# Sigmoid attention and a SwiGLU block on one core: from one head at a time to units of four heads, two side by side in the array

## The chip, the core and the metric

The kernel runs on one core of a Trainium2 chip. A core has a matrix engine (TensorE, PE in the profile; its weight loads are the rows PEld), VectorE (DVE), ScalarE (ACT), GpSimd (POOL) and SyncE (SP), and 16 DMA engines between its memory SBUF and the chip's main memory. Matrix products land in PSUM, eight banks of 2 KB in each of 128 partitions. The metric is the device time of one execution in microseconds.

## The reference, cut to what matters

```python
# q, k, v: (8, 12, 448, 64) float32 ; w_gate, w_val: (768, 1536) ; w_out: (1536, 768)
scores = scale * np.matmul(q, k.transpose(0, 1, 3, 2)) - np.log(S)      # scale = 1/8, S = 448
attn   = 1.0 / (1.0 + np.exp(-scores))                                  # sigmoid, no softmax
attn_out = np.matmul(attn, v)                                           # per batch and head
x = attn_out.transpose(0, 2, 1, 3).reshape(3584, 768)
g = x @ w_gate
silu = g * (1.0 / (1.0 + np.exp(-g)))
out = (silu * (x @ w_val)) @ w_out                                      # (3584, 768) float32
```

## The kernel before, in words

The work goes by batch. Three stages of three batches overlap: in pass `g` the attention of batch `g`, the first feed-forward products (FFN-1: gate and value) of batch `g-1` and the second (FFN-2) of batch `g-2` are written in turns, one head, one column block `f` of FFN-1 and one FFN-2 half per inner step `j` (12 steps a pass). The Tile scheduler then orders the instructions of each engine by its own priorities, so what stands on an engine is not quite what is written.

Tokens are cut into four chunks of 112. `emit_load` (L106) loads a chunk of q, k or v of all twelve heads with one DMA on SyncE's queue; the runs in main memory are 64 floats, 256 bytes. GpSimd casts to 16 bits (L116; for batch 0 ScalarE does, L114). `emit_tr` (L125) transposes q or k of a pair of heads by four TensorE products with the identity into the PSUM buffer `TO`, and VectorE copies it out (L132): a pair's q lies then with one head in partitions 0 to 63 and the other in 64 to 127.

Scores (`emit_qk`, L151): per head four products, one for each chunk of keys, each with 64 rows of contraction (one half of the array's rows) and 112 columns of weights, moving 448 queries. All four of a head use the same half. ScalarE takes the sigmoid out of PSUM (L163, 112x448). `emit_pv` (L168): per head four products with 112 rows and 64 columns of weights (one half of the array's columns, always the first), accumulated into `ps_pv`; VectorE casts them into the half of `xT` that belongs to the head (L185).

FFN-1 (`emit_ffn1_mm`, L194): per block `f` six products for the gate and six for the value, 128x128 weights, 448 moving. ScalarE takes the sigmoid of the gate (L205), VectorE multiplies twice (L207, L209). FFN-2 (`emit_ffn2`, L223): per 112 tokens and 384 output columns twelve products into `TO`, moving 384; ScalarE copies out (L230), and GpSimd's queue stores 112 rows (L235). Transposes and FFN-2 share the one buffer `TO`.

Weights come as 36 tiles of 128x768 floats (L81) through four staging buffers, three at each step, and are cast by ScalarE (L88) and VectorE (L90) in turns.

Of the kernel before, what the change touches and what calls it, by code (L numbers as in the profile page):

```python
# [9 lines left out]
FP32 = mybir.dt.float32  # L10
FP16 = mybir.dt.float16
# [7 lines left out]
def kernel(  # L19
# [15 lines left out]
    PC = 112  # L35
    NC_ = S // PC
    NP = H // 2
    NF = DFF // 128
    HSC = 4096.0
# [5 lines left out]
    psum = ctx.enter_context(tc.tile_pool(name="ps", bufs=1, space=bass.MemoryType.PSUM))  # L45
    stg = ctx.enter_context(tc.tile_pool(name="stg", bufs=1))
    one = ctx.enter_context(tc.tile_pool(name="one", bufs=1))
    two = ctx.enter_context(tc.tile_pool(name="two", bufs=2))
    wp = ctx.enter_context(tc.tile_pool(name="wp", bufs=1))
    attn = ctx.enter_context(tc.tile_pool(name="attn", bufs=4))  # L50
    ptp = ctx.enter_context(tc.tile_pool(name="ptp", bufs=8))
    xtp = ctx.enter_context(tc.tile_pool(name="xtp", bufs=12))
    htp = ctx.enter_context(tc.tile_pool(name="htp", bufs=22))
    osp = ctx.enter_context(tc.tile_pool(name="osp", bufs=2))

    idn = one.tile([PC, PC], BF16, tag="idn")
    make_identity(nc, idn)
    sb_t = one.tile([128, 1], FP32, tag="sbiast")
    nc.gpsimd.memset(sb_t, sbias)

    wg16 = [wp.tile([128, DFF], FP16, tag=f"wg{j}", name=f"wg16_{j}") for j in range(NP)]
    wv16 = [wp.tile([128, DFF], FP16, tag=f"wv{j}", name=f"wv16_{j}") for j in range(NP)]
    wo16 = [wp.tile([128, DM], FP16, tag=f"wo{f}", name=f"wo16_{f}") for f in range(NF)]

    wjobs = []
    for j in range(NP):
        rows = slice(j * 128, (j + 1) * 128)
        for h2 in range(2):
            cols = slice(h2 * DM, (h2 + 1) * DM)
            wjobs.append((moe_w_gate[rows, cols], wg16[j][:, cols]))  # L70
            wjobs.append((moe_w_val[rows, cols], wv16[j][:, cols]))
    for f in range(NF):
        rows = slice(f * 128, (f + 1) * 128)
        wjobs.append((moe_w_out[rows, :], wo16[f][:, :]))
    NWJ = len(wjobs)
    wstage = {}

    def emit_wload(i):
        src, _ = wjobs[i]
        st = stg.tile([128, DM], FP32, tag="wst", bufs=4, name=f"wst{i}")  # L80
        nc.sync.dma_start(out=st, in_=src)  # L81
        wstage[i] = st

    def emit_wcast(i, eng=None):
        _, dst = wjobs[i]
        eng = eng or nc.scalar
        if eng is nc.scalar:
            eng.copy(out=dst, in_=wstage.pop(i))  # L88
        else:
            eng.tensor_copy(out=dst, in_=wstage.pop(i))  # L90

    q16 = {}
    k16 = {}
    v16 = {}

    def get16(d, b, dt, nm):
        if b not in d:
            d[b] = two.tile([PC, NC_, H, D], dt, tag=nm, name=f"{nm}{b}")
        return d[b]

    def emit_load(b, which, c):
        src = (q, k, v)[which]
        nm = ("qst", "kst", "vst")[which]
        st = stg.tile([PC, H, D], FP32, tag=nm, bufs=(4, 4, 3)[which], name=f"{nm}_{b}_{c}")
        sl = slice(c * PC, (c + 1) * PC)
        nc.sync.dma_start(out=st, in_=src[b][:, sl, :].rearrange("h t d -> t h d"))  # L106
        return st

    def emit_cast(b, which, c, st, eng=None):
        d, dt, nm = ((q16, BF16, "q16"), (k16, BF16, "k16"), (v16, FP16, "v16"))[which]  # L110
        t = get16(d, b, dt, nm)
        eng = eng or nc.gpsimd
# [245 lines left out]
```

## Time and profile before

| | before |
|---|---|
| three runs | 640.72, 641.11, 647.34 us (median 641.11) |
| span of the profiled execution | 646.1 us, 5.0 above the median |
| busy: PE, PEld | 610.1, 297.3 us |
| busy: ACT, DVE, POOL | 321.8, 220.9, 85.9 us |
| moved by DMA | 58.71 MB, 131648 packets under 512 bytes |
| products on PE | 3072 |

A row of the timeline has the start, the time from its first start to its last end, the engine, the line, the operation with its tiles (out<-in, contraction*columns of the weights, shape of the moving operand), and how many instructions it merges; in brackets is the idle time before it and what ended it. Products are pipelined: a single one lasts 0.35 us from start to end while the next starts 0.19 us after it, so starts, and not ends, give the pace. A row of the windows has, for a stretch of time, the busy time and the number of instructions of each engine, the granted TensorE clock, the mean share of the DMA engines and the GB/s.

### The profile page before, as it was taken

To read this page: it belongs to the slowest core of one execution; us is meant where nothing else is said; L and a number is where in the kernel's file an instruction comes from. 1 tells how busy PE (TensorE), PEld (TensorE's weight loads), DVE (VectorE), ACT (ScalarE), POOL (GpSimd) and SP (SyncE) were. 2 spreads that over 40 slices of the span, in tenths; PEclk is the share of its full clock that TensorE was granted. 3 is DMA by queue.
4 is the path that set the end of the run, shared out by engine and by line. 5 is a ranking of instruction groups with operands and counts; after the bars stand their busy time and mean duration, and the time that the engine had idled before them with its cause. 6 is when DMAs were issued, how large, how long until landed. Compare 5 with 4: busy or idle time off the path is not lost.

```text
span 646.1 us, 7821 instructions
## 1 busy us (share of the span) xinstructions
PE 610.1 (94%) x3072; PEld 297.3 (46%) x3072; DVE 220.9 (34%) x402; ACT 321.8 (50%) x576; POOL 85.9 (13%) x123
## 2 busy tenths in 40 slices
PE   0899879999999999999999999999999999999985
PEld 0332323344555455444555455544545454546653
DVE  0232326444333432344333433344333433333310
ACT  4767537655545554455445554555445544542221
POOL 0011110351231102210040102110000000000000
PEclk9999999999999999999999999999999999999999
DMA  9956986995695423704092400010010000000112
GB/s 191 203 144 164 231 243 186 208 208 106 137 218 117 102 50 78 136 23 85 22 173 62 87 23 21 22 30 14 22 43 22 1 23 21 22 22 22 44 43 65
DMA packets 138341, 58.71 MB, mean 91 GB/s; under 512 B 131648, under 2 KB 131648, under 8 KB 138304
## 3 DMA queue, kind: packets, MB, share of 16 engines
q1 hardware_dynamic: 135744, 47.19, 35.3%
q0 software_dynamic: 2560, 11.01, 5.5%
q8 instruction: 24, 0.39, 0.3%
q14 instruction: 13, 0.11, 0.1%
HBM read 47.19 MB, written 11.01 MB: 90 GB/s over the span
## 4 chain that ended last, share of the span: by engine, by line
PE 60%; issue 32%; POOL 2%; ACT 2%; SPq 1%; DMA 1%; DVE 1%; POOLq 0%; ACTq 0%
PE ps_sc L151 12%; PE ps_g L194 12%; PE ps_pv L168 12%; PE ps_vl L194 11%; PE ps_o L223 10%; PE ps_tr L125 4%; SPq L106 1%; POOL out_dram L235 1%; DMA kst<-in_k_dram 1%; ACT pt L163 1%; POOL v L116 0%; DVE xT L185 0%; DVE kT L132 0%; ACT wg L88 0%; ACT L163 0%
## 5 line engine op out<-in xcount | busy, mean ns | idle before, releaser
L163 ACT ACTIVATE pt<-ps_sc,sb_t 112x448 f16<-112x448 f32 x384 | 222.4, 636 | 102.2 <-PE ps_sc L151 93.0
L223 PE MATMUL ps_o<-wo,hT 128*112 128x384 f16 x768 | 135.7, 326 | 4.2 <-ACT osb L230 4.2
L194 PE MATMUL ps_g<-xT,wg 128*128 128x448 f16 x576 | 131.7, 361 | 2.2 <-DVE t L207 1.3
L194 PE MATMUL ps_vl<-xT,wv 128*128 128x448 f16 x576 | 129.3, 359 | 0.3 <-DVE t L207 0.3
L151 PE MATMUL ps_sc<-qT,kT 64*112 64x448 bf16 x384 | 121.9, 409 | 2.9 <-ACT pt L163 2.8
L223 PEld LDWEIGHTS <-hT 128*112 128x112 f16 x768 | 99.8, 130 | 35.4 <-issue 5.6
L168 PE MATMUL ps_pv<-pt,v 112*64 112x448 f16 x384 | 110.2, 390 | 1.6 <-ACT pt L163 1.2
L207 DVE TENSOR_TENSOR t<-ps_g,s 128x448 f16<-128x448 f32 x96 | 60.0, 625 | 149.0 <-ACT s L205 148.8
L205 ACT ACTIVATE s<-ps_g 128x448 f16<-128x448 f32 x96 | 52.2, 544 | 91.1 <-PE ps_g L194 89.5
L230 ACT ACTIVATE osb<-ps_o 112x384 f32<-112x384 f32 x64 | 31.4, 491 | 113.5 <-PE ps_o L223 113.5
L194 PEld LDWEIGHTS <-wg 128*128 128x128 f16 x576 | 50.0, 99 | 72.3 <-issue 35.5
L194 PEld LDWEIGHTS <-wv 128*128 128x128 f16 x576 | 50.0, 98 | 68.2 <-issue 31.2
L185 DVE CAST xT<-ps_pv 64x448 f16<-64x448 f32 x96 | 59.3, 617 | 61.0 <-PE ps_pv L168 60.3
L209 DVE SCALAR_TENSOR_TENSOR hT<-ps_vl,t 128x448 f16<-128x448 f32 x96 | 60.0, 625 | 46.7 <-PE ps_vl L194 44.6
L235 POOL DMA_DIRECT2D out_dram<-osb x32 | 17.0, 531 | 364.6 <-ACT osb L230 364.6
L151 PEld LDWEIGHTS <-kT 64*112 64x112 bf16 x384 | 35.8, 133 | 59.3 <-issue 56.9
L168 PEld LDWEIGHTS <-v 112*64 112x64 f16 x384 | 36.4, 114 | 54.1 <-issue 36.5
L132 DVE COPY qT<-ps_tr 128x448 bf16<-128x448 bf16 x48 | 18.7, 389 | 76.2 <-PE ps_tr L125 76.2
L132 DVE COPY kT<-ps_tr 128x448 bf16<-128x448 bf16 x48 | 18.7, 389 | 64.2 <-PE ps_tr L125 64.2
L125 PE MATMUL ps_tr<-idn,q 112*128 112x112 bf16 x192 | 21.6, 233 | 16.4 <-ACT q L114 14.5
L116 POOL CAST q<-qst 112x768 bf16<-112x768 f32 x28 | 22.6, 830 | 86.6 <-DMA qst<-in_q_dram 62.6
L116 POOL CAST v<-vst 112x768 f16<-112x768 f32 x28 | 22.9, 843 | 79.6 <-DMA vst<-in_v_dram 40.6
(20 smaller groups left out, 107.7 us busy)
## 6 DMA issues: line engine op xcount, KB each, us to landing
qst<-in_q_dram SPq DMA_DIRECT2D x32, 336.0 KB, 5.9
kst<-in_k_dram SPq DMA_DIRECT2D x32, 336.0 KB, 6.2
vst<-in_v_dram SPq DMA_DIRECT2D x32, 336.0 KB, 5.6
out_dram<-osb POOLq DMA_DIRECT2D x32, 336.0 KB, 3.0
wst<-in_moe_w_gate_dram SPq DMA_DIRECT2D x12, 384.0 KB, 4.2
wst<-in_moe_w_val_dram SPq DMA_DIRECT2D x12, 384.0 KB, 4.5
wst<-in_moe_w_out_dram SPq DMA_DIRECT2D x12, 384.0 KB, 3.8
```

The costliest lines, as they stand in the source:

```text
L116: eng.tensor_copy(out=t[:, c], in_=st)
L125: nc.tensor.transpose(out=ps[:, c * PC:(c + 1) * PC], in_=src[:, c, 2 * p:2 * p + 2, :], identity=idn,)
L132: nc.vector.tensor_copy(out=t, in_=ps)
L151: nc.tensor.matmul(out=sc, lhsT=kT[ro:ro + D, c * PC:(c + 1) * PC], rhs=qT[ro:ro + D, :], start=True, stop=True,)
L163: nc.scalar.activation(out=pt, in_=sc, func=SIGM, bias=sb_t[:PC], scale=qkscale)
L168: nc.tensor.matmul(out=pv, lhsT=v16[b][:, c, h, :], rhs=pts[c], start=(c == 0), stop=(c == NC_ - 1),)
L185: nc.vector.tensor_copy(out=xT[(b, p)][ro:ro + D, :], in_=pv[0:D, :])
L194: nc.tensor.matmul(out=ps, lhsT=w[j][:, f * 128:(f + 1) * 128], rhs=xT[(b, j)], start=(j == 0), stop=(j == NP - 1),)
L205: nc.scalar.activation(out=s16, in_=gps, func=SIGM)
L207: nc.vector.tensor_tensor(out=t1, in0=gps, in1=s16, op=MULT)
L209: nc.vector.scalar_tensor_tensor(out=ht, in0=vps, scalar=HSC, in1=t1, op0=MULT, op1=MULT)
L223: nc.tensor.matmul(out=o, lhsT=hT[(b, f)][:, tci * PC:(tci + 1) * PC], rhs=wo16[f][:, half * 384:(half + 1) * 384], start=(f == 0), stop=( ...
```

## The change

The kernel is written anew in units of four heads of one batch (24 units `i`, three a batch), each in four slots. `tc.manual_schedule()` keeps on each engine the order in which the code is written.

- **Tokens.** The 448 tokens are cut into 384 and 64. In the 384, partition `p` holds the three neighbouring tokens 3p to 3p+2, so that loads of q, k and v have runs of 192 floats (768 bytes). The last 64 tokens (256-byte runs) of q and k share one tile, q in one half of the partitions and k in the other, the halves changing places with the batch.
- **Transposes.** Seven of 128x128 for a pair of heads (three of k, three of q, one of both tails) where there were eight; one VectorE copy of 832 columns and two of 64x64 that put the two heads' key tails on the diagonal of a 128x128 block `kbd`.
- **Scores.** Per 128 keys, one product for each of two heads: the first head in the upper half of the array's rows, the second in the lower, next to each other in the order and into two banks. The tails of a pair are one product with the full array (`kbd`). One sigmoid covers 128x896.
- **PV.** Per 128 keys, one product for each of two heads, the first in the first half of the columns, the second in the other, into one bank; the tails are one full product with the block-diagonal `vbd`. One VectorE cast of 128x448 empties both heads.
- **FFN-1** keeps its products; weights come in four blocks of 384 columns, as tiles of 128x2x384 (runs of 1536 bytes). FFN-1 of block 0 begins in slot 1 of unit 3.
- **FFN-2** works on pairs of batches, in 28 tiles of 128 tokens instead of 32 of 112, a half of 384 columns in about 14 of 22 slots from unit 9 on. ScalarE empties the first half, VectorE the second. After the attention it takes its PSUM from the scores' two buffers (`late`).
- **Casts.** GpSimd does all but those of unit 0.

The core of the diff, new functions that the prediction speaks of (helper and allocation lines left out):

```diff
+    ctx.enter_context(tc.manual_schedule())
...
+    def load_quad(i):
+        for nm, src in (("q", q), ("k", k), ("v", v)):
+            t = stg.tile([128, 4, NS, D], FP32, tag="st", bufs=10, name=f"st_{nm}{i}")
+            nc.sync.dma_start(
+                out=t,
+                in_=src[b][hs, 0:SM, :].rearrange("h (p s) d -> p h (s d)", s=NS),
+            )
...
+    def emit_tr(i, pp):
+        ps = psum.tile([128, 2 * S], BF16, tag="TO", bufs=1, name="ps_tr")
+        ko, qo, to = (0, SM, 2 * SM) if even else (2 * ST + SM, 2 * ST, 0)
+        for src, off in ((k16[i], ko), (q16[i], qo)):
+            for s in range(NS):
+                nc.tensor.transpose(
+                    out=ps[:, off + s * 128:off + (s + 1) * 128],
+                    in_=src[:, s, hs, :], identity=idn)
+        nc.tensor.transpose(out=ps[:, to:to + 128], in_=qk16[i][:, hs, :], identity=idn)
...
+        nc.vector.tensor_copy(out=m, in_=ps[:, mo:mo + S + SM])
+        for hp in range(2):
+            r = slice(64 * hp, 64 * hp + 64)
+            nc.vector.tensor_copy(out=kb[r, r], in_=ps[r, kt:kt + ST])
...
+    def emit_sc(i, pp, s):
+        sc = psum.tile([128, 2, 512], FP32, tag="A", bufs=2, name="ps_sc")
+        kT, qT, _ = qkT[(i, pp)]
+        for hp in range(2):
+            r = slice(64 * hp, 64 * hp + 64)
+            nc.tensor.matmul(out=sc[:, hp, 0:S], lhsT=kT[r, s * 128:(s + 1) * 128],
+                             rhs=qT[r, :], start=True, stop=True)
...
+    def emit_pv(i, pp):
+        pv = psum.tile([128, S], FP32, tag="P", bufs=1, name="ps_pv")
+        for s in range(NS):
+            for hp in range(2):
+                c = slice(64 * hp, 64 * hp + 64)
+                nc.tensor.matmul(out=pv[c, :], lhsT=v16[i][:, 2 * pp + hp, s, :],
+                                 rhs=pts[(i, pp, s)][:, hp, :], start=(s == 0), stop=False)
+        nc.tensor.matmul(out=pv, lhsT=vbd[i % NVB][:, pp, :], rhs=pts[(i, "t")][:, pp, :],
+                         start=False, stop=True)
...
+    for i in range(nsteps):
+        att = i < NQ
+        for sl in range(4):
+            fg = 4 * (i - QB) - 1 + sl
+            f1 = 0 <= fg < B * NF
+            if f1:
+                gps = emit_f1(fb, ff, wg16, "ps_g")
+                t1 = emit_gate_post(gps)
+            if att:
+                if sl == 0:
+                    jobs = [emit_sc(i, 0, 0), emit_sc(i, 0, 1)]
+                elif sl == 1:
+                    jobs = [emit_sc(i, 0, 2), emit_sct(i)]
+                elif sl == 2:
+                    jobs = [emit_sc(i, 1, 0), emit_sc(i, 1, 1)]
+                else:
+                    jobs = [emit_sc(i, 1, 2)]
+            if sl == 0 and 1 <= i <= NQ:
+                pvj = (i - 1, 1)
+            if sl == 3 and att:
+                pvj = (i, 0)
+            if pvj:
+                pv = emit_pv(*pvj)
+            for jb in jobs:
+                emit_sig(jb)
+            if pvj:
+                emit_pvcast(*pvj, pv)
+            if i + 1 < NQ and sl in (1, 2):
+                emit_tr(i + 1, sl - 1)
+            if f1:
+                vps = emit_f1(fb, ff, wv16, "ps_v")
+                emit_val_post(fb, ff, vps, t1)
+                if ff == NF - 1 and fb % 2 == 1:
+                    f2q.extend((fb // 2, u) for u in range(2 * (2 * NS + 1)))
+            f2acc = f2acc + 14.0 / 22.0 if f2q else 0.4
+            if f2q and f2acc >= 1.0:
+                f2acc -= 1.0
+                emit_f2(*f2q.pop(0))
+            if sl == 0 and i + 2 < NQ:
+                cast_quad(i + 2)
...
+            if sl == 3:
+                if i + 3 < NQ:
+                    load_quad(i + 3)
+                if i < 3:
+                    load_wc(i + 1)
```

How instructions move, at three places. First TensorE in the steady part, at the scores. Before (`ps_g`, `ps_vl` are gate and value, `ps_sc` the scores of one head, `kT` and `qT` the transposed k and q of its pair):

```order
L194 MATMUL ps_g<-xT_5_2815,wg_5_97 128x448
L151 LDWEIGHTS kT_4_3140
L151 MATMUL ps_sc<-qT_4_3072,kT_4_3140 112x448
...
L194 LDWEIGHTS wv_0_98
L194 MATMUL ps_vl<-xT_0_2169,wv_0_98 128x448
```

and in the change, slot 1 of unit 8 (`qkT` holds k and q of a pair, `kbd` the diagonal block of its key tails, `ps_tr` the transposes):

```order
L218 MATMUL ps_g<-xT_5_1143,wg_2_92 128x448
L174 LDWEIGHTS qkT_0_1370
L174 MATMUL ps_sc<-qkT_0_1370 128x448
...
L182 LDWEIGHTS kbd_76
L182 MATMUL ps_sct<-qkT_0_1370,kbd_76 128x448
L182 LDWEIGHTS kbd_77
L182 MATMUL ps_sct<-qkT_1_1411,kbd_77 128x448
L153 LDWEIGHTS k_9_1332
L153 MATMUL ps_tr<-idn,k_9_1332 128x128
```

The scores stood two and two around the gate, both of one head; now the two of a pair of heads stand next to each other, the tails and the seven transposes follow, and only then the value products.

Second, VectorE in the slots with transposes. Before:

```order
L132 COPY kT_3_3001<-ps_tr 128x448
L185 CAST xT_1_3059<-ps_pv 64x448
L207 TENSOR_TENSOR t_3040<-ps_g,s_3038 128x448
L209 SCALAR_TENSOR_TENSOR hT_3_3042<-ps_vl,t_3040 128x448
L132 COPY qT_4_3072<-ps_tr 128x448
```

and in the change:

```order
L226 TENSOR_TENSOR t_1761<-ps_g,s_1759 128x448
L160 COPY qkT_1_1781<-ps_tr 128x832
L163 COPY kbd_77<-ps_tr 64x64 x2
L233 SCALAR_TENSOR_TENSOR hT_1_1792<-ps_v,t_1761 128x448
L255 TENSOR_SCALAR osb_0_1685<-ps_o 128x384
```

The copies that empty `TO` stand now behind the gate's multiplication, in the same slot whose FFN-2 half takes `TO` next.

Third, SyncE's queue at the start. Before (`wst` are weight tiles):

```order
L106 DMA vst_3_138<-in_v_dram 112x12x64
L81 DMA wst_183<-in_moe_w_gate_dram 128x768
L81 DMA wst_185<-in_moe_w_val_dram 128x768
L81 DMA wst_187<-in_moe_w_gate_dram 128x768
L106 DMA qst_0_189<-in_q_dram 112x12x64
L106 DMA kst_0_191<-in_k_dram 112x12x64
```

and in the change, the end of unit 2's load, the first block of weights and the start of unit 3's:

```order
L83 DMA st_v_185<-in_v_dram 128x4x192
L98 DMA sv_187<-in_v_dram 64x2x64 x2
L106 DMA st_wg_0_190<-in_moe_w_gate_dram 128x2x384
...
L106 DMA st_wv_2_200<-in_moe_w_val_dram 128x2x384
L83 DMA st_q_287<-in_q_dram 128x4x192
L83 DMA st_k_289<-in_k_dram 128x4x192
```

Before, all of batch 0 came first and then weights and batch 1 by turns; now units and blocks of weights (six tiles) alternate.

More of the change, by code (lines that the diff above doesn't have):

```diff
@@ L72 @@
[L72 to L86, printed above, removed]
+    NKB = 4
+    kbd = [one.tile([128, 128], BF16, tag=f"kbd{i}", name=f"kbd{i}") for i in range(NKB)]
@@ L87, in emit_wcast, with cp @@
+    def cp(eng, o, i):
         if eng is nc.scalar:
-            eng.copy(out=dst, in_=wstage.pop(i))
+            eng.copy(out=o, in_=i)
         else:
[L90 to L107, printed above, removed]
@@ L331 @@
+    while f2q:
+        emit_f2(*f2q.pop(0))
 _INS = ['q', 'k', 'v', 'moe_w_gate', 'moe_w_val', 'moe_w_out']
```

398 lines of the change are left out of this document (179 added, 219 removed).

## The prediction

> **What bounds the kernel now.** I read the page first, then the windows by stage, then the timeline of TensorE in the steady part, at the start and at the end.
>
> ```profile
> span 646.1 us, 7821 instructions
> PE 610.1 (94%) x3072; PEld 297.3 (46%) x3072; DVE 220.9 (34%) x402; ACT 321.8 (50%) x576; POOL 85.9 (13%) x123
> ...
> 2.00:98.00 96.00, 72.08 (x235) 25.92 (x236) 24.12 (x50) 54.14 (x87) 10.51 (x12) 1.00 0.87 201
> 140.00:560.00 420.00, 420.00 (x2232) 209.02 (x2230) 153.01 (x278) 214.77 (x396) 59.17 (x82) 1.00 0.31 67
> ```
>
> No engine but PE is near its span. From 140 to 560 us PE runs 5.3 products a microsecond without a break; in the first 98 us it runs 2.4 while the DMA engines are 87% busy. So there are two regimes: a long one in which PE's own pace counts, and a start of about 100 us. One head of the long one, by starts:
>
> ```profile
> 307.41 2.11 PE L223 MATMUL ps_o<-wo,hT 128*112 128x384 f16 x12
> 309.46 0.75 PE L168 MATMUL ps_pv<-pt,v 112*64 112x448 f16 x3
> 310.14 0.37 PE L125 MATMUL ps_tr<-idn,q 112*128 112x112 bf16 x4
> 310.45 0.38 PE L168 MATMUL ps_pv<-pt,v 112*64 112x448 f16 x1
> 310.75 0.58 PE L151 MATMUL ps_sc<-qT,kT 64*112 64x448 bf16 x2
> 311.27 1.31 PE L194 MATMUL ps_g<-xT,wg 128*128 128x448 f16 x6
> 312.51 0.58 PE L151 MATMUL ps_sc<-qT,kT 64*112 64x448 bf16 x2
> 313.02 1.31 PE L194 MATMUL ps_vl<-xT,wv 128*128 128x448 f16 x6
> 314.17 2.11 PE L223 MATMUL ps_o<-wo,hT 128*112 128x384 f16 x12
> ```
>
> A head takes 314.17 - 307.41 = 6.76 us and nothing waits. The value products, followed by another full-array group, take 1.15 us for six: 0.19 each. The gate takes 1.24 and is followed by scores on half the rows: such a change of the used part of the array costs about 0.09 at its end. One PV alone takes 0.30 (0.11 over), two scores 0.51 (0.13 over), four transposes 0.31, so about 0.054 each. FFN-2 is (2.05 - 0.09) / 12 = 0.163 a product. A score with 64 rows or a PV with 64 columns costs as much as a full one, and 2 x 4 of them a head are 1.5 us.
>
> The start has a second trait, and the evidence for the change's main idea:
>
> ```profile
> 23.31 0.99 PE L151 MATMUL ps_sc<-qT,kT 64*112 64x448 bf16 x2
> 34.32 0.62 PE L151 MATMUL ps_sc<-qT,kT 64*112 64x448 bf16 x2
> 39.02 1.70 PE L168 MATMUL ps_pv<-pt,v 112*64 112x448 f16 x4
> 40.65 0.99 PE L151 MATMUL ps_sc<-qT,kT 64*112 64x448 bf16 x3
> 94.17 2.40 PE L194 MATMUL ps_vl<-xT,wv 128*128 128x448 f16 x6 [0.26 <-DVE t L207]
> 96.37 2.44 PE L194 MATMUL ps_g<-xT,wg 128*128 128x448 f16 x6
> 98.61 1.47 PE L194 MATMUL ps_vl<-xT,wv 128*128 128x448 f16 x6
> ```
>
> Up to 98.6 us a product takes twice its later time, 2.24 us for six at 96.37, though the granted clock reads 1.00 in the windows; after some 4.4 us of unbroken full products it changes. And at 34.32 two scores end within 0.62 us, the length of a single one, where the two at 23.31 need 0.99, and at 40.65 three fit in 0.99. The short ones are the last of one head and the first of the next, which use different halves of the rows. **So two row halves do run side by side.** No row shows this for column halves.
>
> **The change part by part.** Paces: 0.19, 0.163, 0.06 for a transpose of 128 (0.054 x 128/112), 0.10 for a change of the used array part, 0.05 once for a run of row pairs; a pair of halves counts as one product.
> - Slot 0: gate 1.14, two score pairs 0.38, three PV pairs 0.57, a tail 0.19, value 1.14, three changes 0.30, runs 0.07: 3.79. Slot 1: 2.28 + one pair 0.19 + two tails 0.38 + seven transposes 0.42 + 0.25 = 3.52. Slot 2: 2.28 + 0.38 + 0.42 + 0.25 = 3.33. Slot 3: 2.28 + 0.19 + 0.57 + 0.19 + 0.37 = 3.60. A unit is 14.24, of which FFN-1 9.12 and attention 5.12; four heads cost 4 x 2.41 = 9.6 before (6.76 less 2.05 less 2.30).
> - FFN-2: 28 tiles by 2 halves by 12 x 0.163 = 56 x 1.96 = 109.8; before 64 x 2.05 = 131.2.
> - PE in all: 24 x 5.12 + 96 x 2.28 + 109.8 = 122.9 + 218.9 + 109.8 = **451.6**. By the same paces before: 96 x 2.41 + 218.9 + 131.2 = 581.5, which leaves 64.6 of the span for start and end.
>
> The other engines:
>
> ```profile
> L163 ACT ACTIVATE pt<-ps_sc,sb_t 112x448 f16<-112x448 f32 x384 | 222.4, 636 | 102.2 <-PE ps_sc L151 93.0
> L205 ACT ACTIVATE s<-ps_g 128x448 f16<-128x448 f32 x96 | 52.2, 544 | 91.1 <-PE ps_g L194 89.5
> L230 ACT ACTIVATE osb<-ps_o 112x384 f32<-112x384 f32 x64 | 31.4, 491 | 113.5 <-PE ps_o L223 113.5
> L185 DVE CAST xT<-ps_pv 64x448 f16<-64x448 f32 x96 | 59.3, 617 | 61.0 <-PE ps_pv L168 60.3
> L209 DVE SCALAR_TENSOR_TENSOR hT<-ps_vl,t 128x448 f16<-128x448 f32 x96 | 60.0, 625 | 46.7 <-PE ps_vl L194 44.6
> L132 DVE COPY kT<-ps_tr 128x448 bf16<-128x448 bf16 x48 | 18.7, 389 | 64.2 <-PE ps_tr L125 64.2
> L116 POOL CAST q<-qst 112x768 bf16<-112x768 f32 x28 | 22.6, 830 | 86.6 <-DMA qst<-in_q_dram 62.6
> ```
>
> ACT's 448 and 384 columns differ by 53 ns, 0.83 ns a column, so a sigmoid of 896 is about 0.64 + 0.37 = 1.01; a unit has seven, four gate sigmoids and 1.3 copies: 9.9 us of 19. DVE per unit: eight FFN-1 operations 5.0, two PV casts 1.2 (four halves before), transposes about 2.0, 1.3 copies 0.7: 8.9. POOL: three large casts 2.5 and three small ones, and 5.0 for a weight block in each of the first units, of 14. All stay under PE, so what they lose or gain costs nothing, with one exception. The 832-column copy lies between 0.39 and 0.72 us (448 columns, and in proportion); I take 0.6 since a fixed part is surely in the 0.39, and 0.2 for each small copy.
>
> ```profile
> 305.86 0.54 ACT L205 ACTIVATE s<-ps_g 128x448 f16<-128x448 f32 x1 [0.55 <-PE ps_g L194]
> 306.44 0.62 DVE L207 TENSOR_TENSOR t<-ps_g,s 128x448 f16<-128x448 f32 x1 [1.71 <-ACT s L205]
> ```
>
> In slots 1 and 2 DVE first waits for the gate's sigmoid: 0.6 + 0.6 + 1.1 of copies, 2.3 us after the gate's end. PE wants `TO` for FFN-2 about 2.2 us after that end in slot 1 and 2.0 in slot 2. So FFN-2 **waits 0.1 and 0.3 us**, in 64% of the slots of 15 units: 4 us. Bounds: 0 and, with copies of 1.5, 8. Queued behind it is only the next gate.
>
> **The start.** Unit 3's FFN-1 begins behind the transposes of unit 3, and in the same slot stand those of unit 4, so PE passes there once unit 4's q and k are in. SyncE's order puts five units and two weight blocks ahead: 5 x 1.38 + 2 x 2.36 = 11.6 MB.
>
> ```profile
> 0.74 0.37 SPq L106 DMA_DIRECT2D qst<-in_q_dram  x1
> 18.30 1.36 PE L151 MATMUL ps_sc<-qT,kT 64*112 64x448 bf16 x3
> ...
> 5.00:10.00 5.00, 0.55 (x2) 0.21 (x2) 0.00 (x0) 2.64 (x4) 0.00 (x0) 1.00 1.33 213
> 90.00:95.00 5.00, 4.74 (x12) 1.23 (x11) 1.78 (x4) 1.90 (x3) 0.83 (x1) 1.00 0.95 295
> ```
>
> Runs of 256 bytes alone give 213 GB/s; a stretch mostly of 3072-byte rows gives 295. The new runs are 768 and 1536 bytes; between 213 and 295 I take 280, nearer to the long ones. 11.6 MB take 41.5 us (39.3 to 54.5); 2 us of start and 1 of casting are about what v of unit 4, not needed yet, gives back. **PE passes at 42 us** (40 to 55). Until then units 0 to 2 need at most 3 x 9.5 us at the doubled pace from about 9 us on (one unit is enough where 18.30 needed a whole batch), 40 with slot 0: hidden by the loads. By then PE has done 3 x 5.12 + 1.5 + 2.0 = 18.9 of its work, so 42 - 18.9 = 23.1 are lost. Later loads hold nobody up: a unit with a weight block is 3.74 MB, 13.4 us, under PE's 14.2; at 213 GB/s it would be 17.6, and some 3 us a unit for five units come on top.
>
> The doubled pace after that: 94.17 to 98.61 says 4.4 us, so 2.2 lost, if nothing interrupts; 14 if a whole unit passes so. I take 4. The Trainium skill, page "TensorE: Matmul & The Clock Gate", section "Part 1: The HAM clock gate (the "warmup" mystery)", says that about 3.4 us of sustained activity open the clock. The rows from 34.32 to 40.65 disagree as far as half-array products go, which follow each other there for more than that at the slow pace; by that rule of the Trainium skill the attention units would soon run at 0.19 and my 4 would be nearly 0.
>
> **The end.**
>
> ```profile
> 635.36 2.11 PE L223 MATMUL ps_o<-wo,hT 128*112 128x384 f16 x12 [0.58 <-ACT osb L230]
> 638.10 2.11 PE L223 MATMUL ps_o<-wo,hT 128*112 128x384 f16 x12 [0.63 <-ACT osb L230]
> ```
>
> With one buffer each of the last FFN-2 halves waits 0.6 for its copy; with two these waits go. From the last product's end, 640.1, to the span's end, 6.0 stay.
>
> **Sum**: 451.6 + 23.1 + 4 + 4 + 6.0 = 488.7 of span. The span shown is 646.1 where the runs' median is 641.1, a factor of 0.992: **485 us**.
>
> **Rivals.**
> 1. *Column halves do not overlap.* For: no row shows it; both halves need all rows and write one bank. Against: the row halves overlap in the same array. Price: 144 PV pairs x 0.19 = 27 us: 512. A half-way case lies between. In the Trainium skill, the same page, section "Part 3: Packing small matmuls — row/col tiling", three column tiles gave 2.38 instead of 3; a pair at that efficiency would cost, as an estimate, 144 x 0.19 x 0.26 = 7 us: 492. No run here shows column tiles side by side.
> 2. *The doubled pace lasts.* For: it lasted 98 us before, through many FFN-1 products. Against: there PE was broken up by waits for weights; here full products follow densely. One to two units more are 14 to 28 us: 500 to 513.
> 3. *The halves do not overlap at all*, so the change does not do what it says: 27 more for scores, 539. Against: 34.32.
> 4. *Slower than before*: in the written order every wait of PE for a load stops all, and the doubled pace never goes away. Price 1 us for each us of work; from 156 of the remaining 433 us on the change loses; with all of it, about 900. Against: from 140 us on every row stands at 0.19 with half-array products among them.
>
> **How the numbers follow.** Forecast 0.71 (its own range 470 to 498), rival 1 0.12, rival 2 0.12, rival 3 0.03, rival 4 0.02. Low end: the start at 40, no waits for `TO`, 2 for the pace: 481 of span, 477, less 7 for changes of array part that a pair may hide: 470. High end: rival 1, rival 2 or a start at 55: 514. A measurement of this kernel can tell about 1% from no change; all but rival 4 lie far below 635: faster 0.97, same 0.01, slower 0.02.
>
> **What would show it.** Right: scores and PV of a pair starting within some 10 ns; slots of 3.3 to 3.8 us without FFN-2; no wait of PE over 0.5 us from unit 4 on; PE passing the transposes of unit 4 near 42 us; sigmoids near 1.0 us. Wrong: PV products 0.19 apart (rival 1); products of 0.37 after 55 us (rival 2); the transposes waiting for casts in units 4 to 8; a mean wait of FFN-2 for `TO` over 0.5 us.

## The result and the profile after

| | before | changed |
|---|---|---|
| median of four runs each, same chip | 644.12 us (640.72 to 647.34) | 480.0 us (478.24 to 481.07) |
| ratio, 95% interval | | 0.744 [0.740, 0.748] |
| profiled execution, its span | 646.1 us span | 481.07 us, span 479.3 |

The change takes a quarter off the time. 485 was forecast, within 470 to 514.

The page of the changed kernel: span, busy time and instructions of each engine, the GB/s in the 40 slices of 12 us, and the DMA packets.

```profile
span 479.3 us, 7353 instructions
PE 455.2 (95%) x2832; PEld 223.6 (47%) x2832; DVE 207.1 (43%) x421; ACT 221.0 (46%) x295; POOL 125.0 (26%) x216
GB/s 233 307 340 327 330 333 332 260 182 106 115 52 133 0 149 148 42 142 115 82 100 117 34 120 92 85 83 36 33 2 33 34 34 33 21 46 34 33 100 98
DMA packets 68578, 58.67 MB, mean 122 GB/s; under 512 B 22208, under 2 KB 65216, under 8 KB 68544
```

PE's busy time fell by 154.9 us, the span by 166.8: PE is still the engine that counts, and the other 11.9 us are time in which it stood idle. The bytes are the same, the packets under 512 bytes a sixth of those before, and the loads run at some 330 GB/s from 24 to 84 us. Four windows (columns as before):

```profile
0.00:20.00 20.00, 10.24 (x59) 4.69 (x59) 6.13 (x22) 10.84 (x11) 8.77 (x22) 1.00 0.91 255
20.00:40.00 20.00, 13.25 (x99) 5.54 (x95) 7.25 (x18) 16.42 (x19) 14.13 (x20) 0.99 1.08 329
40.00:60.00 20.00, 19.20 (x108) 8.88 (x109) 9.42 (x20) 8.55 (x11) 14.94 (x23) 0.84 1.07 338
140.00:420.00 280.00, 279.84 (x1754) 137.69 (x1753) 126.08 (x248) 129.93 (x177) 48.95 (x91) 1.00 0.24 73
```

The regime without a break, which began at 100 us before, begins at about 41. From 140 to 420 us PE idles for 0.16 us; POOL, ACT and DVE are nowhere near full.

Unit 4 on PE, from the timeline: one slot in full, then the gates that open the next ones.

```profile
51.88 1.30 PE L218 MATMUL ps_g<-xT,wg 128*128 128x448 f16 x6
53.11 0.55 PE L174 MATMUL ps_sc<-qkT 64*128 64x448 bf16 x4
53.59 0.76 PE L198 MATMUL ps_pv<-pt,v 128*64 128x448 f16 x6
54.28 0.36 PE L200 MATMUL ps_pv<-pt,vbd 128*128 128x448 f16 x1
54.48 1.30 PE L218 MATMUL ps_v<-xT,wv 128*128 128x448 f16 x6
55.62 1.30 PE L218 MATMUL ps_g<-xT,wg 128*128 128x448 f16 x6
...
59.06 1.30 PE L218 MATMUL ps_g<-xT,wg 128*128 128x448 f16 x6
...
62.31 1.30 PE L218 MATMUL ps_g<-xT,wg 128*128 128x448 f16 x6
...
65.86 1.30 PE L218 MATMUL ps_g<-xT,wg 128*128 128x448 f16 x6
```

Four scores now take 53.59 - 53.11 = 0.48 us, where two took 0.51 before; six half-column value products take 0.69, three times a single pace and a change. In the single records of such a group the two products of a pair start 2 to 4 ns apart and the next pair 189 to 210 ns later: column halves overlap as fully as row halves. The slots last 3.74, 3.44, 3.25 and 3.55 us, together 13.98.

The start on PE, from the same view:

```profile
16.93 1.33 PE L198 MATMUL ps_pv<-pt,v 128*64 128x448 f16 x6
...
19.47 0.76 PE L198 MATMUL ps_pv<-pt,v 128*64 128x448 f16 x6
...
40.80 0.50 PE L153 MATMUL ps_tr<-idn,k 128*128 128x128 bf16 x3 [4.30 <-POOL k L122]
...
41.52 2.45 PE L218 MATMUL ps_v<-xT,wv 128*128 128x448 f16 x6
43.76 2.45 PE L218 MATMUL ps_g<-xT,wg 128*128 128x448 f16 x6
...
47.20 1.30 PE L218 MATMUL ps_v<-xT,wv 128*128 128x448 f16 x6
...
445.86 27.46 PE L250 MATMUL ps_ol<-wo,hT 128*128 128x384 f16 x168
```

The doubled pace ends near 19 us, in the middle of attention (1.33 at 16.93, 0.76 at 19.47). The transposes of unit 4 pass at 40.80, after 4.30 us of waiting for GpSimd's cast of k, and for the next 5.7 us PE is back at 2.24 us for six. The windows (columns as before) show it as well, where they are cut to fit:

```profile
39.70:43.10 3.40, 2.30 (x12) 1.41 (x13) 0.88 (x3) 0.00 (x0) 2.50 (x5) 0.50 1.03 344
43.10:46.50 3.40, 3.40 (x13) 1.11 (x11) 0.62 (x1) 0.25 (x1) 2.94 (x5) 0.50 1.02 342
```

The granted clock is 0.50 in both, and 1.00 from 46.5 on. Its first recorded change is at 19.2 us (at 98.9 in the kernel before); ahead of that the windows read 1.00 though the products run at the doubled pace. At the end the last product is over at 445.86 + 27.46 = 473.3, 5.9 before the span's end.

### The profile page after: what moved, and what is told of

The parts are those of the page before. It is cut to its first block, busy times and chain, and to the rows that moved or that the text cites. A ratio compares the mean times of both kernels' runs of the same rounds, so it can differ in the third digit from the quotient of the medians.

```text
span 479.3 us, 7353 instructions
## 1 busy us (share of the span) xinstructions
PE 455.2 (95%) x2832; PEld 223.6 (47%) x2832; DVE 207.1 (43%) x421; ACT 221.0 (46%) x295; POOL 125.0 (26%) x216
## 4 chain that ended last, share of the span: by engine, by line
PE 88%; DMA 6%; SPq 1%; issue 1%; DVE 1%; ACT 1%; POOL 0%; POOLq 0%
PE ps_g L218 23%; PE ps_v L218 22%; PE ps_o L250 16%; PE ps_ol L250 7%; PE ps_sc L174 7%; PE ps_pv L198 6%; PE ps_tr L153 3%; DMA st_k<-in_k_dram 3%; PE ps_pv L200 3%; PE ps_sct L182 2%; DMA st_wg<-in_moe_w_gate_dram 1%; DMA st_q<-in_q_dram 1%; DMA sv<-in_v_dram 1%; DVE t L226 1%; SPq L98 1%
## 5 line engine op out<-in xcount | busy, mean ns | idle before, releaser
L188 ACT ACTIVATE pt<-ps_sc,sbiast 128x896 f16<-128x896 f32 x144 | 138.7, 1004 | 2.5 <-PE ps_sc L174 2.5
L218 PE MATMUL ps_v<-xT,wv 128*128 128x448 f16 x576 | 125.8, 355 | 0.0
L226 DVE TENSOR_TENSOR t<-ps_g,s 128x448 f16<-128x448 f32 x96 | 60.0, 625 | 148.2 <-ACT s L224 148.2
L250 PEld LDWEIGHTS <-hT 128*128 128x128 f16 x672 | 64.5, 98 | 48.2 <-DVE kbd L163 4.9
L250 PE MATMUL ps_o<-wo,hT 128*128 128x384 f16 x456 | 80.5, 327 | 0.0
L233 DVE SCALAR_TENSOR_TENSOR hT<-ps_v,t 128x448 f16<-128x448 f32 x96 | 60.0, 625 | 32.4 <-PE ps_v L218 28.8
L263 POOL DMA_DIRECT2D out_dram<-osb x24 | 13.2, 552 | 230.7 <-DVE osb L255 115.0
L174 PE MATMUL ps_sc<-qkT 64*128 64x448 bf16 x288 | 46.1, 368 | 2.9 <-ACT pt L188 2.6
L198 PE MATMUL ps_pv<-pt,v 128*64 128x448 f16 x288 | 37.0, 365 | 0.0
L250 PE MATMUL ps_ol<-wo,hT 128*128 128x384 f16 x216 | 35.9, 326 | 0.0
L160 DVE COPY qkT<-ps_tr 128x832 bf16<-128x832 bf16 x48 | 28.2, 588 | 17.0 <-PE ps_tr L156 17.0
L207 DVE CAST xT<-ps_pv 128x448 f16<-128x448 f32 x48 | 30.0, 625 | 12.7 <-PE ps_pv L200 11.0
```

The costliest lines, as they stand in the source:

```text
L160: nc.vector.tensor_copy(out=m, in_=ps[:, mo:mo + S + SM])
L174: nc.tensor.matmul(out=sc[:, hp, 0:S], lhsT=kT[r, s * 128:(s + 1) * 128], rhs=qT[r, :], start=True, stop=True)
L188: nc.scalar.activation(out=pt, in_=sc[:, :, 0:S], func=SIGM, bias=sb_t, scale=qkscale)
L198: nc.tensor.matmul(out=pv[c, :], lhsT=v16[i][:, 2 * pp + hp, s, :], rhs=pts[(i, pp, s)][:, hp, :], start=(s == 0), stop=False)
L207: nc.vector.tensor_copy(out=t, in_=pv)
L218: nc.tensor.matmul(out=ps, lhsT=w[c][:, j, ff * 128:(ff + 1) * 128], rhs=xT[(b, j)], start=(j == 0), stop=(j == KC - 1))
```

## Experiments

Each was timed beside the kernel before on the same chip; the changed kernel's 480.0 is the yardstick. Times are medians of four runs. The groups of runs were on four chips, on which the kernel before has medians of 645.3 to 647.4 (644.12 beside the changed kernel), so a difference of 1 or 2 us from 480.0 says nothing.

| what is altered | expected over 480 (theory) | us | over 480.0 |
|---|---|---|---|
| PV head by head | +18 | 480.28 | 0 |
| scores head by head | +9 | 479.08 | -1 |
| PV of the heads apart by the gate | +32 | 511.57 | +31.6 |
| scores of the heads apart by the gate | +40 | 520.74 | +40.7 |
| score pairs in two places | +8 | 489.02 | +9.0 |
| FFN-2 tiles of 112 | +16 | 497.97 | +18.0 |
| short load runs | +8 to +12 | 494.31 | +14.3 |
| order left to the scheduler | +7 | 479.05 | -1 |
| unit 4 loaded earlier | -5 to -7 | 483.64 | +3.6 |
| the same with four buffers of v | -5 to -7 | 474.29 | -5.7 |
| that one under the scheduler | +0 to +4 on 474.3 | 484.17 | +9.9 on 474.3 |
| that one, halves apart in units 0 to 2 | +16 to +18 on 474.3 | 490.31 | +16.0 on 474.3 |

**Must the two products of a pair be neighbours?** First the value products:

```diff
-        for s in range(NS):
-            for hp in range(2):
+        for hp in range(2):
+            for s in range(NS):
```

> The same products, but PV of a pair is written head by head: three with the first half of the columns, then three with the second. Only the third and the fourth can then run side by side, so a call has five product times instead of three. Theory (the column halves overlap and TensorE sets the time): 48 calls x 2 x 0.19 = +18 us on the changed kernel, and within a call steps of 0.19 except one near 0.003. Rival (the gain comes from fewer and larger instructions elsewhere, the pairs are not what counts): 0 to +3.

Measured: 480.28, ratio 0.744 [0.739, 0.749]. The theory, that neighbours alone can pair, is wrong. The time is the rival's, but its reason is not: the pairs are still there. The timeline of this kernel, one group:

```profile
304.46 0.77 PE L198 MATMUL ps_pv<-pt,v 128*64 128x448 f16 x6
305.16 0.36 PE L200 MATMUL ps_pv<-pt,vbd 128*128 128x448 f16 x1
```

Six products in 0.70 us, though three of the first head are written first and three of the second behind. In the single records they start at 304.460 and .470, .674 and .684, .863 and .873: pairs 10 ns apart. Two products of one half never start so close (in the kernel before, whose value products all use the first half, never under 189 ns), so the first product of the second head has started past two waiting ones of the first.

The same for scores: the new function writes two key blocks of one head, then the same two of the other.

```diff
-                    jobs = [emit_sc(i, 0, 0), emit_sc(i, 0, 1)]
+                    jobs = emit_sc2(i, 0, 0)
```

> The same products, but in slots 0 and 2 the four scores are written head by head (first head, two blocks of keys, then the second head), so that four take three product times instead of two. Theory (row halves overlap, TensorE sets the time): 48 slots x 0.19 = +9 us on the changed kernel. Rival (ScalarE's sigmoids or the order sets the pace of these slots): 0 to +2. A side question is when the pace of 0.19 first appears: in the changed kernel it does so near 18.5 us, in the kernel before near 98; if only products that fill the array count for that, it should come later here.

Measured: 479.08, ratio 0.741 [0.737, 0.745], pairs 6 ns apart in the records. Again no loss. The side question has its answer too: the pace of 0.19 begins near 17 us, not later than in the changed kernel. Neighbours in the written order are not what makes a pair.

**What does unmake it?** Both times the products of the first head were moved to before the gate and those of the second (with the tail) left behind it, so that six products on the whole array lie between.

```diff
+            if pvj:
+                pv = emit_pv(*pvj, 0, None)
             if f1:
                 gps = emit_f1(fb, ff, wg16, "ps_g")
...
-                pv = emit_pv(*pvj)
+                pv = emit_pv(*pvj, 1, pv)
```

> Writing PV head by head cost nothing, and in its trace the two halves still started together. So the first theory, that only neighbours in the order overlap, has fallen; the new one is that each half takes its next product as soon as it is free, past waiting products of the other half, as long as no full-array product lies between. Here the first head's three PV products stand ahead of the gate's six full products and the second head's behind them, in the 42 calls of slots with FFN-1. New theory: nothing overlaps there, 42 x (3 x 0.19 + 0.2 for one more run of half-array products) = +32 us on the changed kernel. Rival (the pairs never mattered, only changes of the array part and sizes do): 42 x 0.2 = +8.

```diff
+            firsts = [emit_sc(i, pp, s, 0) for pp, s in mine[sl]] if att else []
             if f1:
                 gps = emit_f1(fb, ff, wg16, "ps_g")
...
+                jobs = [emit_sc(*key, 1, sc) for key, sc in firsts]
```

> The same for the scores: the first head's products stand ahead of the gate, the second head's behind it, in all slots with FFN-1 and attention, 83 of them. New theory (row halves overlap only without full products between): 40 x 0.38 + 41 x 0.19 + 83 x 0.2 = +40 us. Rival (only the additional changes cost): 83 x 0.2 = +17.

Measured: 511.57 (ratio 0.794 [0.789, 0.800]) and 520.74 (0.809 [0.803, 0.814]), both where the theory had put them. In the timeline of the kernel with PV apart:

```profile
306.57 0.75 PE L198 MATMUL ps_pv<-pt,v 128*64 128x448 f16 x3
307.26 1.31 PE L220 MATMUL ps_g<-xT,wg 128*128 128x448 f16 x6
...
308.80 0.76 PE L198 MATMUL ps_pv<-pt,v 128*64 128x448 f16 x3
309.48 0.36 PE L202 MATMUL ps_pv<-pt,vbd 128*128 128x448 f16 x1
```

Three half products cost 0.69 us ahead of the gate and three more 0.68 behind it, where all six took 0.69. With scores apart one product is 0.30 on each side of the gate:

```profile
303.50 0.36 PE L174 MATMUL ps_sc<-qkT 64*128 64x448 bf16 x1
303.80 1.31 PE L218 MATMUL ps_g<-xT,wg 128*128 128x448 f16 x6
305.04 0.36 PE L174 MATMUL ps_sc<-qkT 64*128 64x448 bf16 x1
305.33 0.55 PE L182 MATMUL ps_sct<-qkT,kbd 128*128 128x448 bf16 x2
```

So a half passes waiting products of the other half but not those of the whole array. Nor those of the other split: in units 0 to 2 of the kernel with PV apart only scores, on row halves, lie between, and the value products don't pair there either.

```profile
25.73 0.76 PE L198 MATMUL ps_pv<-pt,v 128*64 128x448 f16 x3
26.42 0.36 PE L174 MATMUL ps_sc<-qkT 64*128 64x448 bf16 x2
26.71 0.76 PE L198 MATMUL ps_pv<-pt,v 128*64 128x448 f16 x3
```

Against an order with such products between, the order of the pairs is worth 31.6 us for PV and 40.7 for scores. All 144 pairs of PV are lost in the records, 27.4 us by 0.19, and 129 of the 144 of scores, 24.5. Both kernels also change the array part more often, 329 and 405 times where the changed kernel does 239 times, which is 9.9 and 18.3 us by the 0.11 of the next run. These sums, 37.3 and 42.8, are above what was measured; part of the difference is the start, where PE's wait for unit 4 is 1.12 and 2.14 us instead of 4.30, and with PV apart no doubled pace follows it.

**What does a change of the array part cost?** One of the two score pairs of slots 0 and 2 goes ahead of the gate. PE's order has then 321 changes between products of different parts instead of 239 (the kernel before had 588).

```diff
+            if att and sl in (0, 2):
+                jobs = [emit_sc(i, sl // 2, 0)]
             if f1:
                 gps = emit_f1(fb, ff, wg16, "ps_g")
...
-                    jobs = [emit_sc(i, 0, 0), emit_sc(i, 0, 1)]
+                    jobs.append(emit_sc(i, 0, 1))
```

> The same products and pairs, but in slots 0 and 2 one score pair stands ahead of the gate and one behind it, as the kernel before had it, which makes 321 changes between used parts of the array instead of 239. Theory (each change costs about 0.1 us on the path): 82 x 0.1 = +8 us, so that the 588 changes of the kernel before explain some 35 us of the whole gain. Rival (changes are hidden, other waits take their place): 0 to +2.

Measured: 489.02, ratio 0.757 [0.753, 0.761], +9.0 for 82 changes: 0.11 us each, with pairs intact. In the single records of the changed kernel a change adds 0.09 to 0.10 (starts 278 to 294 ns apart where 189 to 200 are usual), so about 8 of the 9.0 are the changes themselves.

**FFN-2 in tiles of 112 again.**

```diff
-            nc.tensor.matmul(out=o, lhsT=hT[(m, f)][:, t * 128:(t + 1) * 128],
+            nc.tensor.matmul(out=o, lhsT=hT[(m, f)][:, t * 112:(t + 1) * 112],
...
-                    f2q.extend((fb // 2, u) for u in range(2 * (2 * NS + 1)))
+                    f2q.extend((fb // 2, u) for u in range(16))
```

> FFN-2 goes back to 112 tokens a tile, 64 halves instead of 56, spread over 16 of 22 slots; the stores go to consecutive rows, so the rows of the output are in another order than the reference's. Theory (each half costs its twelve products and nothing else): 8 x 1.96 = +16 us, a little more with further waits for the shared transpose buffer. Rival (the weight loads of 112 columns, 130 ns instead of 98, show as well): 768 x 0.03 = +23 more. Rival (hidden behind other work): 0.

The rows of the output then stand in another order of the tokens; the work is that of 32 tiles. Measured: 497.97, ratio 0.770 [0.765, 0.775], +18.0. The costliest groups of the changed kernel and, behind them, of this one:

```profile
L250 PEld LDWEIGHTS <-hT 128*128 128x128 f16 x672 | 64.5, 98 | 48.2 <-DVE kbd L163 4.9
```

```profile
L250 PEld LDWEIGHTS <-hT 128*112 128x112 f16 x768 | 98.2, 130 | 33.4 <-DVE kbd L163 7.2
```

96 products more at 0.163 are 15.6; the other 2.4 us are not traced. A weight load of 112 columns takes 130 ns instead of 98, still under the 163 of a product, so the rival that laid more on it falls.

**The loads.** Runs of 256 bytes again, in 128-token blocks; the tokens of a partition are then other ones, consistently in loads and stores, and everything else stays.

```diff
-            nc.sync.dma_start(
-                out=t,
-                in_=src[b][hs, 0:SM, :].rearrange("h (p s) d -> p h (s d)", s=NS),
-            )
+            for s in range(NS):
+                nc.sync.dma_start(
+                    out=t[:, :, s, :],
+                    in_=src[b][hs, s * 128:(s + 1) * 128, :].rearrange("h p d -> p h d"),
+                )
```

> The 384 tokens are cut into three blocks of 128 neighbours instead of every third token, so that q, k and v load in runs of 256 bytes as before; each tile takes three DMAs instead of one, 13 issues a unit instead of 7. Theory (the start is bound by the bytes ahead of unit 4's k and q): at 213 GB/s for these loads a unit takes 6.5 us instead of about 4.2, five of them 11 more, so TensorE passes the transposes of unit 4 near 51 us instead of 40.8, and the time is +8 to +12 us. Rival (the start is bound by casts or ScalarE, the run length does not matter): 0 to +2. Rival (the loads hold up later units as well): +15 and more.

Measured: 494.31, ratio 0.765 [0.760, 0.771], +14.3, between the theory and the rival of +15. From its timeline:

```profile
38.09 0.50 PE L154 MATMUL ps_tr<-idn,k 128*128 128x128 bf16 x3 [8.26 <-POOL k L123]
...
53.32 0.50 PE L154 MATMUL ps_tr<-idn,k 128*128 128x128 bf16 x3 [6.45 <-POOL k L123]
...
54.04 2.45 PE L219 MATMUL ps_v<-xT,wv 128*128 128x448 f16 x6
```

PE passes unit 4's transposes at 53.32 instead of 40.80, 12.5 us later, and each of the two long waits is followed by a stretch at the doubled pace. One later wait for a cast of k, 1.66 us ahead of 112.98, which the changed kernel doesn't have, is about the rest: the theory's start carries the loss, and the rival's later unit adds a little.

**The order left to the scheduler.**

```diff
-    ctx.enter_context(tc.manual_schedule())
```

> The written order alone is undone: the same instructions, ordered by the Tile scheduler's priorities. In its order there are 287 changes of the used array part instead of 239, and some ten PV calls are broken up. Theory (the order counts only through changes and broken pairs): 48 x 0.1 + about 12 x 0.19 = +7 us, and the start about the same. Rival (the written order is what keeps TensorE from waiting): +20 and more.

Measured: 479.05, ratio 0.743 [0.737, 0.747]: neither. It has 287 changes of the array part, 48 more, which by 0.11 are 5.3 us; and nine pairs are broken up, 1.7 by 0.19. Against that, PE's gaps over 0.6 us sum to 10.2 us instead of 14.9, since it puts other products where the written order stands still, and the doubled pace does not come back, which saves 2.7. These estimates nearly cancel.

**Can the wait at 40.80 be taken away?** By loading unit 4 ahead of the second weight block and casting it a unit earlier. `load_quad(3)` goes with unit 0 and `load_quad(i + 4)` from there on; GpSimd casts weights a little later.

```diff
+            if sl == 3 and i == 1:
+                cast_quad(4)
...
-                if i + 3 < NQ:
-                    load_quad(i + 3)
+                if i == 0:
+                    load_quad(3)
+                if i + 4 < NQ:
+                    load_quad(i + 4)
```

> Unit 4's q, k and v are loaded and cast ahead of the second block of weights, and so on with each later unit and block; nothing else changes. Theory (TensorE's wait of 4.3 us for unit 4 and the slow pace from 40.8 to 46.1 behind it come from the order of the loads): unit 4 is in by about 32 us, the wait goes, and so does the slow stretch that follows it: -5 to -7 us on the changed kernel. Rival (the second block of weights or a later unit is then late by as much): 0. Rival (the slow pace stays, as the pace depends on something other than the wait): -3 to -4.

Here, with three buffers for v, unit 4's tail of v goes into unit 1's buffer before the last product with that tail in unit 1 is issued, so a part of the output is made from the wrong tail. Measured: 483.64, ratio 0.749 [0.745, 0.753], +3.6, a miss. The timeline:

```profile
37.19 0.56 PE L200 MATMUL ps_pv<-pt,vbd 128*128 128x448 f16 x1 [11.25 <-POOL vbd L122]
```

PE stood 11.25 us for unit 4's tail of v, whose buffer the tail of unit 1 uses. The wait had not gone but moved, to a buffer. With a fourth one (`NVB = 4`, `bufs=4` for `v16`), which also makes the output the reference's again:

> The loads of unit 4 ahead of the second block of weights again, with four buffers each for v and for the block-diagonal v tails instead of three: with three, unit 4's tail of v went into the buffer that unit 1 still needed, in value and in time (TensorE waited 11.3 us for it, and the output of unit 1 was made from unit 4's tail). Theory: no wait over 1.5 us and no slow stretch after 18 us: -5 to -7 us on the changed kernel, 473 to 475. Rival (another load takes its place): 0.

Measured: 474.29, ratio 0.737 [0.731, 0.743], 5.7 under the changed kernel: its four runs (473.12 to 475.33) lie below all four of the changed kernel. The timeline around the place of the old wait:

```profile
33.72 1.30 PE L218 MATMUL ps_g<-xT,wg 128*128 128x448 f16 x6
...
35.63 0.33 PE L153 MATMUL ps_tr<-idn,k 128*128 128x128 bf16 x3
...
36.02 1.30 PE L218 MATMUL ps_v<-xT,wv 128*128 128x448 f16 x6
```

No wait, and the value product at 36.02 runs at once at the single pace: the doubled pace after 40.80 was the price of the wait ahead of it, not of FFN-1's beginning. On this version the scheduler was tried once more:

> The kernel of the run before, ordered by the Tile scheduler instead of as written. With the changed kernel's loads the scheduler's order made no difference in the whole (479.05 against 480.0): it had fewer waits in the start and more changes of the array part. Theory (these two cancel, and with earlier loads the written order has no waits left to lose): 0 to +4 on the run before. Rival (the scheduler fills other gaps as well): -3.

Measured: 484.17, ratio 0.752 [0.747, 0.758], +9.9: a miss. It has 309 changes, 70 more (7.7 us by 0.11), and in its start the pairs are broken up; the doubled pace lasts until 28 instead of 17.6:

```profile
14.68 0.58 PE L197 MATMUL ps_pv<-pt,v 128*64 128x448 f16 x1
...
27.27 0.96 PE L197 MATMUL ps_pv<-pt,v 128*64 128x448 f16 x3
28.16 0.36 PE L173 MATMUL ps_sc<-qkT 64*128 64x448 bf16 x2
```

So the written order is worth 10 us there and nothing with the loads of the change.

**What ends the doubled pace?** In units 0 to 2 of the four-buffer version a tiny product on the whole array (8 columns) separates the two heads:

```diff
+    def emit_apart(i, keys):
+        for hp in range(2):
+            if hp == 1:
+                divide(scs[0][:, 0, S:S + 8])
+            for (pp, s), sc in zip(keys, scs):
...
+                nc.tensor.matmul(out=pv[:, 0:8], lhsT=zero, rhs=idn[:, 0:8],
+                                 start=False, stop=(hp == 1))
```

> The version with unit 4's loads earlier (474.29 us, span 471.3), but in units 0 to 2 the products of the two halves are kept apart by a tiny product on the whole array (8 columns; behind the first head's scores, and behind each head's three PV products, where it adds zeros), and the tail of PV comes first. The output stays the reference's. From unit 3 on nothing changes. In units 0 to 2 a unit has then 24 products that use half of the array, one after another, 4 full ones, 14 transposes and 8 tiny ones. Theory: only products that fill the array bring TensorE to the fast pace, as the first 98 us of the kernel before suggest. Then 0.37 us a product last through the three units: 28 x 0.37 + 14 x 0.11 + 8 x 0.18 = 13.3 us a unit, 40 from 9.1 us on, so FFN-1 begins at about 49 instead of 33.7, with its first groups at 2.4 us for six for some 5 us more: 16 to 18 us over, 490 to 492. Rival: a few microseconds of products of any kind are enough. Then the pace changes near 19 us as in that version, a unit takes 28 x 0.19 + 14 x 0.06 + 8 x 0.1 = 7.0 after the first one's 13, FFN-1 begins at 36 to 38, at once at 1.3 us for six, and the time is 3 to 4 us over: 477 to 478.

Measured: 490.31, ratio 0.760 [0.752, 0.767], +16.0. The four runs lie far apart (485.34 to 492.07). The time is the theory's by luck, for the timeline is neither's:

```profile
26.67 1.27 PE L218 MATMUL ps_pv<-pt,v 128*64 128x448 f16 x3
...
27.99 0.36 PE L191 MATMUL ps_sc<-qkT 64*128 64x448 bf16 x1
...
30.74 0.35 PE L191 MATMUL ps_sc<-qkT 64*128 64x448 bf16 x1 [0.55 <-ACT pt L205]
...
31.14 0.93 PE L191 MATMUL ps_sc<-qkT 64*128 64x448 bf16 x2
...
38.94 0.76 PE L218 MATMUL ps_pv<-pt,v 128*64 128x448 f16 x3
...
50.41 1.29 PE L246 MATMUL ps_g<-xT,wg 128*128 128x448 f16 x6
```

Half products do bring the single pace: after 14 us of them, from 13.2 on, at 27 to 28. It goes again at 31.1, after waits of 0.22 and 0.55 us (waits of 0.28, 0.55 and 0.47 between 42 and 46 us do not end it), comes back after 7 us near 38.2 (three value products in 0.76 at 38.94) and then holds until FFN-1 at 50.41, which runs at 1.29 from its first group. In the four-buffer version, with pairs, it comes at 17.6 and survives a wait of 0.54 at 22.4 and one of 1.11 before 28.66. That pairs matter for the pace is shown; by which rule is not.

Behind the long waits the records of the granted clock show more than the starts. In all runs its changes lie whole multiples of 3.41 us apart (39.69 and 46.52 in the changed kernel), and in every run with pairs in the start it goes back to 1.00 at the end of the first whole step without a long wait. From the end of such a wait that took 3.5 to 5.7 us here, by where in a step it ended.

## Why the prediction was right

Term by term, the prediction's working against the trace (PE's share is counted from starts):

| term | predicted | measured | from |
|---|---|---|---|
| a unit without FFN-2 | 14.24 us | 13.98 | slots of unit 4 |
| attention in 24 units | 122.9 | 116.6 | 24 x (13.98 - 9.12) |
| FFN-2 | 109.8 | about 109 | 0.162 a product |
| passing the transposes of unit 4 | at 42 | at 40.80 | timeline |
| lost by then | 23.1 | 22.7 | 40.80 - (3 x 4.86 + 1.5 + 2.0) |
| doubled pace after it | 4 | 2.7 | 41.1 to 47.2 |
| waits for `TO` | 4 | 1.0 | 7 of 0.136 and 7 of 0.011 |
| end | 6.0 | 5.9 | 473.3 to 479.3 |
| sum of the span | 488.7 | 479.3 | |

With FFN-1's 218.9 the measured terms sum to 476.8. Of the 2.5 left over, 1.6 are five gates behind the attention that start 0.32 us late, waiting for VectorE's multiplication (L226); the sum had no term for them.

The sum itself was 9.4 us of span too high. That 485 came nearer is luck: the factor of 0.992, taken from the median and one profiled execution of the kernel before, took 3.9 us off, while here the time is 1.8 above the span of the same execution (481.07 and 479.3).

- **The pairs** carry the gain, as the sum has it. That column halves overlap, the step with no row to rest on, came out on the full side: rival 1 (512) and rival 3 (539) fall. With scores or PV apart the time was 520.74 and 511.57.
- **The slots** were 0.26 us a unit too dear, 6 us in all, the largest miss of the sum. The paces of 0.19, 0.10 and 0.06 hold; the 0.05 added for each run of row pairs doesn't: in the single records the two of a pair start 3 ns apart and the next pair follows 197 ns later.
- **The start** came 1.2 us early by errors that offset each other. The loads ran faster than the 280 GB/s taken, and by the page's slices (233, 307 and 340 GB/s for 36 us, then 327) the 11.6 MB were in at about 39, where 43.5 had been reckoned (41.5 and 2 of start). But PE passes 1.6 us after that, not 1.5 before it: GpSimd's timeline has the cast of unit 4's k, for which PE waits, begin only at 39.92, when that load is in, and it takes 0.83. The version with 256-byte runs passes at 53.32, within the 40 to 55 set as bounds.
- **The doubled pace** returned as forecast, but two things about it were wrong. The forecast took it as lasting from the start until FFN-1, as before; it had gone near 19, in attention. And it came back only because of the wait at 40.80: without that wait there is none, and 5.7 us are gained. The rule of the Trainium skill that was weighed there (page "TensorE: Matmul & The Clock Gate", section "Part 1: The HAM clock gate (the "warmup" mystery)", some 3.4 us of sustained activity) was right that the attention units would run at 0.19. Behind the waits the trace agrees with it: one whole step of 3.41 us without a long wait brings the pace back, 5.7 us after the wait that ends at 40.80. It does not cover the single half products here, which took 7 to 14.
- **Waits for `TO`**: predicted at 0.1 and 0.3 us. The waits of the weight loads, with their sum, number and longest:

```profile
PEld L250 <- DVE kbd L163: 4.9, 14, 0.4
```

  The named releaser is the last copy that empties `TO`, and 0.4 the longest. Behind 7 of these 14 waits the first FFN-2 product starts some 325 ns after the product ahead of it, where 189 is usual, and behind the other 7 some 200: 1.0 us in all instead of 4. In most slots nothing waits, so both the size and the number were taken too high.
- **The other engines** were rightly put at nothing. The sigmoid of 896 columns was forecast at 1.01 us, the copy of 832 at 0.6:

```profile
L188 ACT ACTIVATE pt<-ps_sc,sbiast 128x896 f16<-128x896 f32 x144 | 138.7, 1004 | 2.5 <-PE ps_sc L174 2.5
...
L160 DVE COPY qkT<-ps_tr 128x832 bf16<-128x832 bf16 x48 | 28.2, 588 | 17.0 <-PE ps_tr L156 17.0
```

- **Rival 4** falls with the windows: a wait for a load did bring the doubled pace back, for 5.7 us and not for good. With that rival 2 falls too: no product stands at 0.37 after 47 us.

Where the 166.8 us of span came from: 231.4 for attention (96 x 2.41) became 116.6; FFN-2's 131.2 became 109; the start, the waits and the end, 64.6, became 34.8. In attention 768 half products became 288 pairs and 96 full products for the tails, 384 paces of 0.19 or 73 us less; 349 changes of the array part went (by the 0.11 measured, 38). Of the 3.4 left, about 2 are transposes (384 of 0.054 became 336 of 0.056); the others are not traced.

## What to carry over

Small products that fill half of TensorE's array cost half as much here when two that use different halves run together: they need not be neighbours, but no product on the whole array, or on the other split, may be written between them. Next comes the number of changes between parts of the array, about 0.1 us each here, so group what uses the same part. Where PE waits several microseconds for loads at the start, a wait costs its own length and the doubled pace behind it; before a load is moved forward, ask whose buffer its cast takes.

## What the runs showed of the hardware

- TensorE's halves run down their own products: one of the second half started ahead of two of the first that stood before it (of one with scores), 10 ns and 6 ns after the first product, with no loss in time. A product of the whole array stops both (+31.6 and +40.7 us). The Trainium skill, page "TensorE: Matmul & The Clock Gate", section "Part 3: Packing small matmuls — row/col tiling", says that products start strictly in the order of the program; these two runs disagree.
- The doubled pace came back after waits of 4.30 us, of 8.26 and 6.45 us, but not after 1.23 and 1.11. Where single half products followed each other it came back once behind 0.22 and 0.55 us close together, and not behind 0.28, 0.55 and 0.47. From the end of the wait it lasted 5.7 us in the changed kernel, 5.1 and 3.6 with short runs, and 7 where single half products followed.
- The granted clock changes at multiples of 3.41 us. The 0.84 that the windows read for 40 to 60 us is 6.5 of the 20 at 0.50. Ahead of its first recorded change they read 1.00, up to 19.2 us here, while the starts show the doubled pace: there only the starts tell.
- Two weight loads differ by shape alone: 98 ns for 128 columns, 130 for 112.
